# A fused delta-rule attention and soft mixture-of-experts kernel: second layer, slot sum, output products and stores by halves of the columns, with 128-row output products and 48 stores

## The chip, the core and the metric

The kernel runs on one core of one Trainium2 chip. The metric is the device time of one execution in microseconds (us); the figure to compare is the median of several runs. Engines are called as in the profile: PE (TensorE matmul), PEld (TensorE weight load), DVE (VectorE), ACT (ScalarE), POOL (GpSimd), SP (SyncE, which here only issues DMAs).

## The reference, cut to what matters

```python
# q, k, v: (4, 8, 768, 48), beta: (4, 8, 768)
for t in range(S):                                   # delta rule, one state per batch and head
    y[:, :, t] = einsum('bhd,bhde->bhe', q[:, :, t], state)
    v_old = einsum('bhde,bhd->bhe', state, k_n[:, :, t])
    state = state + bt * einsum('bhd,bhe->bhde', k_n[:, :, t], v[:, :, t] - v_old)
x = y.transpose(0, 2, 1, 3).reshape(3072, 384)
logits = x @ phi                                     # phi: (384, 32), 8 experts of 4 slots
slot_input = softmax(logits, axis=0).T @ x           # (32, 384)
for e in range(8):                                   # w1: (8, 384, 1024), w2: (8, 1024, 384)
    slot_out[e] = relu(slot_input[e] @ w1[e]) @ w2[e]
out = softmax(logits, axis=1) @ slot_out             # (3072, 32) @ (32, 384), float32
```

## The kernel before, in words

All arithmetic is float32. The sequence of 768 steps is cut into 12 chunks of 64 (`n`), taken in pairs (`g`). `get` loads k and q of a pair, transposes them on PE and forms Gram products (`gram`), which ACT copies out (`evP`, `evR`, `evB`, all through the helper `copy`, L178) and DVE masks (`mskA`, L365). `invert(g)` then solves a triangular system of the pair by many small DVE steps: it begins with one large transpose (`spread`, L383), goes through a reciprocal (L390) and a long row of `col` and `sub` steps, and ends with another transpose (`backT`, L447). `step(n)` carries the state from chunk to chunk on PE, ACT and DVE; `turn_y` and `route` make the logits, the running slot sums and the transposed combine weights `cT`. When all 12 chunks are through, the mixture-of-experts part follows, and this is where the change lies:

- `first` (L828): slot inputs times w1, for two groups of four experts (`qq`) and two halves of the hidden columns; `turnh` (L846) transposes the hidden layer.
- `second` (L862): hidden layer times w2. One call `snd{qq}.{u}` is 8 products of 384 columns, four experts side by side in four column groups of the array, all added into one PSUM bank `pso`. There are 8 calls.
- `evs` (L871, ACT) copies the bank out, `sum` (L873, PE) adds the four expert rows with a selection matrix, `so` (L874, DVE) divides by the softmax sums. The result is the 32 slots by 384 columns, four times over 32 rows each.
- `om` (L888, PE): the output product. Its weights are 96 columns of `cT` in one of four row groups of 32 rows, and 384 columns of `so` move: 8 calls of 4 products, each into a bank of its own, for 96 output rows each.
- `evo` (L893): 32 copies of 96x384 out of PSUM, half on ACT and half on DVE.
- `st` (L902): 16 stores of 96 partitions by 768 floats (two output rows that lie side by side, 3072 bytes), 10 issued by SP and 6 by POOL.

Every operation is recorded by name with its engine and then issued in an order written out as a table (`ORDER`); each engine takes its operations in that order and waits for what an operation needs. `BANKS` gives each PSUM tile its bank. The weight loads (names beginning with w, L776 and L817, all on SP) have a second table, `GATES`: a load waits besides for a named earlier operation. The lines of the tables' use:

```python
        for i in numbers(ORDER) or range(len(self.ops)):
            self.ops[i].fn()
            last[i] = tc.nc.cur_bb.bb.instructions[-1]
            if i in gates:
                tc.add_manual_dep(last[i], last[gates[i]].name, ...)
```

Of the kernel before, what the change touches and what calls it, by code (L numbers as in the profile page):

```python
# [17 lines left out]
    "#)##%x#&#-#%#3#+#*#(#2#,#'#$#E#D#=#F$K#6#>#.#?#7#G$e#@#O#A#B#C#8$|#P#H#<#4#Q#9#V#I#:#5#;#R#J$d#/#S#T"  # L18
    "#K#L$G#M#0#N$C#W$L$H$D$I#U$E$J$f#X$F#Y#Z$g#[$;#]#^$?#_&1$<#`$@#a$r#b#c$A$s#e#d$N#f#g#h$O%y#i$B$Y$P#j"
    "$=$Z#k#l$h#m$M$>$i$t#n$j#o&0$u#p#q$k$v#r#s#t$l#u&P$z#v$w#w$x#x$y#y$p${$m$n#z&Q$o#{%z$[#|%{#}$Q$q$]'~"  # L20
    "#~$^$#$R$$$%&2$&'}&3$'$S$b$_$`$a&l#1$($)$W&R$T$U&S$-$V$*&k$}'%$~$c%#%$%%%&%'%(%)%*%+%,$+$.%.%/%0%-%1"
    "(#%2%3%4%5%6%7%8&y%9$,%:$2$3%;&z%<%=$1%>%?&#$5%@$4%A%B%C%|&$%D&%$X&a%}(R%E$/%~%F&b%G%H(Q%I&&%J$0&(&'"
    "%K&T&)%L&*&U&V%M&+&_%N(t&,$8%O&`(s%P$6%Q&W%R$7%S(S%T&-%U$9&4$:%V&i&.%W&X&/%X%Y&c%Z&]&j&Y%[&Z%]&[&5&o"
    "&g%^&d&^)/&e&f%_)0&6&p%`&h&9%a&7&8%b%c&>%d&m%e&?%f&B%g&n&:&w&C%h*B&;%i&D%j&x%k%l($%m&<&I&q*A&=&H&@(%"
    "%n%o&K&v%s&{&A&u)E&r&E&|%u&}%t(r&F'$&G%v%w&~(;(q&s&t'#'&%p()%r%q&J''(*'(')'*(&*u'+','-)%(''.(w(('2'/"
    ")&*C'1(.+9(x)#*t(/(+'0'3'4'5(u'6(8'7'8(v+:(:'9(9':)3';(,'<(-(2)4'=)='>(3(0'?+R(4&L'@)>+Q'A&M'B(T*v)$"
    "'C'D(>(1'E(y(?'F'G'H(5(z'I({(U(|(}'J(~(V(6).'K(7'L)'(W'M(X'N(l)-)+'O)((_'P)))*'Q'R(`'S(c),(Y(d'T(e&N"
    "'U(Z*D&O'V,e(k'W*E+G'X)1+H'Y,d)2'Z);'[([)<']'^+='_(j'`(]-[(<(^'a(i-](a'b(='c(b(@'d+>'e'f)?(A'g(C(B'h"
    "'i(I(H(D)C'j(f(J)@'k)A(K'l(E)D(L(F'm(g+7(M'n)B(o'o(h(G)5(p'p'q(N+8*I)9'r)6(O)7)8(P*[*J's't)F'z-:'x+h"
    "'|'{-;)G*F):)H'y)I)J'u)K*G)L*H)M)N*K)R'v)O,f)P)Q*L*Y*M)S*_*X)T)U'w)V+;*`)W*N)X+<)Y*P)Z*O)[*Q)]*R)^+?"  # L30
    "*S)_)`*T)a*U+@)b+A*w-<)c+P+B)d*V+E)e*W*]+D+F)f+C+O*x*^+I)g)h*Z)i+M)j+J+U+K)k+L*y)l+V+N*|)m*z*{)n+%)o"
    "+^)p+&+S*}+_+))q/*+T)r*~+*)s++)t+W+#)u/++0)v+$)w+X+'+[)x,g+()y+/+,)z+Y+`){+--Z+]+1+a)|(m+Z+.)}+b(n)~"
    "-t,h-u,l*#+f*$+c-Y*a+d*%+e*&+i+5+6+3*'+41/*b*(,m*)+2/^+g-`**+j*+-j+k+l*,-a+m/]*--^-k+n*.-h*/-_+o*0-i"
    "*1+p*21-+q*3+r*4*5+s*6+t*<*9*8*7+v+w+x..+y,i*:+z+{*;*=+|+}+u+~,#,n,j,$,k/_,%,&,',(,q,),o*>,p,*,|,+,r"
    ",,*?,u,-*@,s,{,.-l,v,/,w,0,t,1-b-p,2-m-n,3/,-%-c,4,x-o,5-&-s,6,y-=,7,z-q-f-d,8-e-B-r,9->-#,:-$-C-'-g"
    "/}*c,;*e-(,<*d*g*f*k,=*h/|-)*i,>-,-+,?,~-*,@-1,A,}*j.$,B-?,C.%,D-x,E-@-v,F-A-y,G-G1,-w,H.&,I-H-D,J.'"
    ",K1.,L-z-R,M-Q,N,O-E.(-{,P-|,Q-},R-F,S-K.#.)-I.*,T.+,U-L./-M.,-~-U-J17-T,V-V.0.-.1-N.2.3-W10,W-O.4-2"
    ".5/--X,X-P-S16/2.6,_,[,Z/.11.7,Y/3,a,^.814.9,].:,`//0S,b,c.<*l.=/4/0.>/1.?*m0R.@.;.A/~.B.C.D.E/715.F"
    "/5.G/6/8.H/9/B.I--13/;/:.J/G-..K/<-/.L/H12.M/=/D.N/A.O/>.P/`/?1=.Q0T/@/C.R.S.T1;.U/a.V1</b.W.X.Y.Z.["
# [85 lines left out]
def kernel(  # L125
# [11 lines left out]
    nc = tc.nc  # L137
# [795 lines left out]
```

## Time and profile before

| | |
|---|---|
| median of 3 runs | 316.62 us (315.55 to 317.04) |
| the profiled execution | 319.18 us, of which the span of its instructions is 317.5 us |
| mean granted TensorE clock | 0.901 |
| busy in the span | PE 245.4, DVE 215.0, ACT 174.0, POOL 100.1 us |
| DMA | 45.08 MB, mean 142 GB/s; HBM written 4.72 MB (the output) |

The profile is one execution. Times in its views are counted from the span's start. Rows of the chain of waits give start, length and what ran; rows of a table of stretches give each engine's busy time in the stretch, with the count of instructions, then the granted clock, the share of time the 16 DMA engines were busy, and what they moved. In a timeline the bracket gives the idle time before an instruction and what ended it.

### The profile page before, as it was taken

How to read it: one execution, taken by the hardware profiler on the slowest of the kernel's cores; microseconds unless marked ns; L12 is line 12 of the kernel's file. 1: busy time of each engine (PE TensorE's matmuls, PEld its weight loads, DVE VectorE, ACT ScalarE, POOL GpSimd, SP SyncE). 2: the span in 40 equal slices, each digit the busy share in tenths (PEclk: the TensorE clock that was granted, in tenths of full speed). 3: DMA queues.
4: the chain of work that ended last, by engine and by line, in shares of the span. 5: the costliest groups of instructions: out<-in, count | busy, mean ns of one | idle time of the engine just before them, and what ended most of it. 6: DMA issues, size and time to landing. Idle time of an engine off the chain costs nothing.

```text
span 317.5 us, 13695 instructions
## 1 busy us (share of the span) xinstructions
PE 245.4 (77%) x5910; PEld 187.7 (59%) x5910; DVE 215.0 (68%) x584; ACT 174.0 (55%) x420; POOL 100.1 (32%) x215
## 2 busy tenths in 40 slices
PE   0768458879798887889759897787878988998930
PEld 0666347768786756678558586656747874343400
DVE  3378899996498989888899988848793306011630
ACT  1464824687777586878457677533448643201530
POOL 8920017354086005940069501690030000000210
PEclk9978956998999999999878997958879999999975
DMA  7989890395376264024930545966695789970396
GB/s 103 138 111 131 112 129 6 62 124 74 55 100 95 35 100 79 8 51 78 170 89 5 96 145 142 239 204 202 196 372 177 217 281 378 323 255 2 98 306 192
DMA packets 86956, 45.08 MB, mean 142 GB/s; under 512 B 78352, under 2 KB 78480, under 8 KB 86896
## 3 DMA queue, kind: packets, MB, share of 16 engines
q1 hardware_dynamic: 83856, 41.94, 58.5%
q0 software_dynamic: 896, 1.87, 2.2%
q8 instruction: 46, 0.75, 1.1%
q10 hardware_dynamic: 2144, 0.39, 1.0%
q14 instruction: 14, 0.11, 0.1%
HBM read 39.47 MB, written 4.72 MB: 139 GB/s over the span
## 4 chain that ended last, share of the span: by engine, by line
PE 56%; ACT 16%; DVE 8%; issue 6%; DMA 5%; SPq 4%; POOL 1%; POOLq 0%; DVEq 0%; ACTq 0%
ACT sb L178 15%; PE pb L571 6%; PE pb L621 6%; PE pb L327 5%; PE pb L588 5%; PE pb L559 4%; PE pb L862 3%; PE pb L828 3%; PE pb L346 3%; PE pb L495 3%; PE pb L888 3%; PE pb L602 3%; PE pb L469 2%; DMA sb<-in_q_dram 2%; PE pb L515 2%
## 5 line engine op out<-in xcount | busy, mean ns | idle before, releaser
L178 ACT ACTIVATE sb<-pb 128x384 f32<-128x384 f32 (+5 forms) x252 | 113.8, 467 | 72.0 <-PE pb L588 15.5
L531 POOL TENSOR_SCALAR sb<-sb 128x48 f32<-128x48 f32 x160 | 60.7, 405 | 23.9 <-DVE sb L412 14.2
L420 DVE TENSOR_TENSOR sb<-sb 128x31 f32<-128x31 f32 (+15 forms) x155 | 53.8, 347 | 4.3
L425 DVE TENSOR_TENSOR sb<-sb 128x31 f32<-128x31 f32 (+15 forms) x155 | 53.0, 342 | 4.4
L178 ACT ACTIVATE sb<-pb,sb 128x256 f32<-128x256 f32 (+1 forms) x96 | 39.7, 450 | 21.9 <-PE pb L571 7.8
L484 POOL TENSOR_SCALAR sb<-sb 128x512 f32<-128x512 f32 x10 | 16.6, 1667 | 91.9 <-DVE sb L447 23.2
L327 PE MATMUL pb<-sb 128*128 128x128 f32 x192 | 33.1, 317 | 13.0 <-DMA sb<-in_k_dram 9.0
L327 PEld LDWEIGHTS pb<-sb 128*128 128x128 f32 x192 | 24.8, 162 | 16.7 <-issue 10.4
L346 PE MATMUL pb<-sb 48*64 48x128 f32 (+1 forms) x896 | 28.6, 269 | 6.4 <-ACT sb L178 4.9
L571 PE MATMUL pb<-sb 64*64 64x48 f32 x768 | 28.9, 228 | 4.0 <-DVE sb L365 1.6
L571 PEld LDWEIGHTS pb<-sb 64*64 64x64 f32 x768 | 26.3, 143 | 6.7 <-DVE sb L365 1.8
L346 PEld LDWEIGHTS pb<-sb 48*64 48x64 f32 x896 | 23.5, 142 | 10.4 <-ACT sb L178 7.3
L515 PE MATMUL pb<-sb 64*64 64x48 f32 x768 | 29.1, 229 | 0.6 <-issue 0.6
L621 PE MATMUL pb<-sb 128*64 128x96 f32 x352 | 22.1, 274 | 6.8 <-ACT sb L178 4.0
L588 PE MATMUL pb<-sb 64*64 64x96 f32 x384 | 22.4, 258 | 6.2 <-issue 3.5
L515 PEld LDWEIGHTS pb<-sb 64*64 64x64 f32 x768 | 26.2, 143 | 0.8 <-issue 0.7
L621 PEld LDWEIGHTS pb<-sb 128*64 128x64 f32 x352 | 17.8, 152 | 12.1 <-ACT sb L178 4.7
L902 POOL DMA_DIRECT2D out_dram<-sb x6 | 3.2, 534 | 64.5 <-DVE sb L893 62.1
L588 PEld LDWEIGHTS pb<-sb 64*64 64x64 f32 x384 | 18.2, 140 | 8.8 <-ACT sb L178 4.3
L365 DVE TENSOR_TENSOR sb<-pb,sb 128x512 f32<-128x512 f32 x24 | 16.6, 690 | 9.2 <-ACT sb L178 7.8
L559 PE MATMUL pb<-sb 128*64 128x96 f32 x352 | 19.7, 254 | 3.2 <-ACT sb L178 2.0
L561 DVE TENSOR_TENSOR sb<-sb,pb 128x384 f32<-128x384 f32 x22 | 12.1, 552 | 11.1 <-PE pb L559 7.1
(114 smaller groups left out, 327.2 us busy)
## 6 DMA issues: line engine op xcount, KB each, us to landing
sb<-in_moe_w_dram SPq DMA_DIRECT2D x24, 512.0 KB, 5.0
sb<-in_moe_w_dram SPq DMA_DIRECT2D x32, 384.0 KB, 5.1
sb<-in_q_dram SPq DMA_DIRECT2D x24, 192.0 KB, 4.7
out_dram<-sb SPq DMA_DIRECT2D x10, 288.0 KB, 7.2
sb<-in_v_dram SPq DMA_DIRECT2D x24, 96.0 KB, 3.4
sb<-in_v_dram SPq DMA_DIRECT2D x48, 48.0 KB, 3.3
sb<-in_k_dram SPq DMA_DIRECT2D x22, 96.0 KB, 3.3
sb<-in_k_dram SPq DMA_DIRECT2D x44, 48.0 KB, 3.0
```

The costliest lines, as they stand in the source:

```text
L178: S_.activation(o, i, ACT.Copy, **kw)
L327: nc.tensor.transpose(F1(ps)[:, P * h:P * h + P], A(src)[:, x:x + P], ident())
L346: mm(A(ps)[ha(e), i, P * h:P * h + P].rearrange("p (a t) -> p a t", a=2)[:, pr[0]:pr[-1] + 1], x[hd(i), j, h, e], y[hd(i), j, h, e, pr[0]: ...
L365: V.tensor_tensor(o, x4(1), m.unsqueeze(1).unsqueeze(1).broadcast_to([P, 2, HQ, C]), op=ALU.mult)
L420: V.tensor_tensor(p(), v3(tt)[:, j:j + 1, 0:m].broadcast_to(sh), v3(lb)[:, j:j + 1, j + 1:32].rearrange("p x i -> p i x").broadcast_to(sh) ...
L425: V.tensor_tensor(t, t, p(), op=ALU.subtract)
L515: mm(F1(pY[n, j])[ha(1 - e), D * x:D * x + D], A(AA[n])[ha(e), a:a + C], A(UB[n])[ha(e), c:c + D], start=n == 0 and x == 0)
L531: G_.tensor_scalar(y, y, A(nb)[:, c:c + 1], 0.5, op0=ALU.mult, op1=ALU.mult)
L559: mm(bank(pK)[ha(e), j, 2 * D * h:2 * D * h + 2 * D], t4(n, 0)[:, j, 2 * b + h, e], bd()[:, j, b, h, e])
L571: mm(bank(pU[b])[ha(e), j, y:y + D], A(TW[g])[ha(e), a:a + C], A(R)[ha(e), c:c + D], start=x == 4 * b and j == 0)
L588: mm(bank(pU[b])[ha(e), :, y:y + D], A(BBb[g])[ha(e), a:a + C], A(U)[ha(e)].rearrange("p (j x d) -> p x j d", j=2, d=D)[:, x], start=False)
L621: mm(F1(pY[n, j])[ha(1 - e), 2 * D * h:2 * D * h + 2 * D], t4(n, 1)[:, j, h, e], bd()[:, j, h // 2, h % 2, e], start=h == 0)
```

## The change

1. `second` works on 192 columns at a time (`HC`), with a bank for each half (`pso[d]`, the two banks that held the state sums). There are 16 calls `snd{d}.{qq}.{u}`, and `evs`, `sum`, `so` exist once for each half. The table puts half 1 ahead of half 0.
2. `om{d}.{mp}.{cj}` has 128 columns of `cT` as weights and 192 columns of `so[d]` moving; two such products (`e`) stand side by side in one bank, both in the same row group `cj`. There are 24 calls of 2 products. `evE` writes `cT` in another order of columns for it, with the same number of elements.
3. `evo` is 24 copies of 128x384, 12 on ACT and 12 on DVE.
4. `st` is 48 stores of 128 partitions by 192 floats (768 bytes, half an output row each), 24 on SP and 24 on POOL.
5. `ORDER`, `BANKS` and `GATES` are new throughout, for the front of the kernel too.

The code, with the closing part of the old version left out:

```diff
-            A(cT).rearrange("p (x a q m) -> p m x q a", a=2, q=16, m=NG)[:, m],
-            F1(pe2)[:, 0:P].rearrange("p (x q a) -> p x q a", q=16, a=2)), r=[pe2], w=[(cT, m)])
+            A(cT).rearrange("p (e m y) -> p m e y", e=2, y=C)[:, m],
+            F1(pe2)[:, 0:P].rearrange("p (e y) -> p e y", e=2)), r=[pe2], w=[(cT, m)])
...
-    pso = pl.ps()
+    HC = Dm // 2
+    pso = [Buf(x, 1, True) for x in H2]
+    sj = [Buf(rt[1] + HC * x, HC) for x in H2]
+    so = [Buf(rt[0] + HC * x, HC) for x in H2]
+    obs = [Buf(w1b[e, kk].addr + Dm * x, Dm) for e in range(3, 7) for kk in range(NKT) for x in H2]
+    def second(qq, u, d):
         def prod():
             for t in (2 * u, 2 * u + 1):
                 for j in range(4):
-                    mm(F1(pso)[32 * j:32 * j + 32, 0:Dm],
+                    mm(F1(pso[d])[32 * j:32 * j + 32, 0:HC],
                        A(hTb[qq])[:, P * t + 32 * j:P * t + 32 * j + 32],
-                       A(w2b[4 * qq + j, u])[:, Dm * (t % 2):Dm * (t % 2) + Dm], start=qq == 0 and t == 0)
+                       A(w2b[4 * qq + j, u])[:, Dm * (t % 2) + HC * d:Dm * (t % 2) + HC * d + HC], start=qq == 0 and t == 0)
+    def put(d):
+        for qq in H2:
+            for u in range(4):
+                second(qq, u, d)
+        ACTO("evs%d" % d, HC, lambda: S_.copy(A(sj[d]), F1(pso[d])[:, 0:HC]), r=[pso[d]], w=[sj[d]])
+        p4 = pl.ps()
+        PE("sum%d" % d, 560, lambda: mm(F1(p4)[:, 0:HC], A(csel), A(sj[d])), rec=4, r=[csel, sj[d]], w=[p4])
+        DVE("so%d" % d, HC, lambda: V.tensor_scalar(
+            A(so[d]), F1(p4)[:, 0:HC], A(sS)[:, 3:4], None, op0=ALU.mult), r=[p4, (sS, 2)], w=[so[d]])
+        for mp in range(NG // 2):
+            for cj in range(4):
+                c, j = divmod(cj, 2)
+                po, ob = pl.ps(), obs.pop(0)
+                def om(mp=mp, cj=cj, po=po):
+                    r = slice(32 * cj, 32 * cj + 32)
+                    for e in H2:
+                        a = HD * e + P * mp
+                        mm(F1(po)[:, HC * e:HC * e + HC], A(cT)[r, a:a + P], A(so[d])[r])
+                PE("om%d.%d.%d" % (d, mp, cj), 340, om, rec=8, r=[cT, so[d]], w=[po])
+                (DVE if cj % 2 else ACTO)("evo%d.%d.%d" % (d, mp, cj), Dm, ..., r=[po], w=[ob])
+                for e in H2:
+                    def st(c=c, j=j, e=e, mp=mp, ob=ob):
+                        b = 2 * (1 - e) + j
+                        o = out[b * S:b * S + S, HC * d:HC * d + HC].rearrange("(m c y) d -> c m y d", c=2, y=C)
+                        (G_ if e else nc.sync).dma_start(out=o[c, 2 * mp:2 * mp + 2], in_=A(ob)[:, HC * e:HC * e + HC])
+                    DMA("st%d.%d.%d.%d" % (d, mp, cj, e), 0.9, st, 290, eng="POOL" if e else "SP", r=[ob])
+    for d in H2:
+        put(d)
```

Where the tables move instructions is shown at three places, as rows of an engine's order: line, operation, operands, shape, and how many of the kind stand in a row. The lines of the new version are one higher than the old ones up to L857 (L862 became L868, L873 became L880, L888 became L892, L902 became L900).

PE at the end of the program, before: second layer (L862), hidden transposes (L846), one transpose of `route` (L717), `sum` (L873), `om` (L888).

```order
L862 MATMUL pb<-sb 32x384 x8
L846 MATMUL pb<-sb 128x128 x4
L862 MATMUL pb<-sb 32x384 x24
L846 MATMUL pb<-sb 128x128 x4
L862 MATMUL pb<-sb 32x384 x16
L717 MATMUL pb<-sb 128x128
L862 MATMUL pb<-sb 32x384 x8
L873 MATMUL pb<-sb 128x384
L888 MATMUL pb<-sb 96x384 x32
```

The same place now, from the last hidden transpose on (L847), with the second layer L868, `sum` L880 and `om` L892.

```order
L847 MATMUL pb<-sb 128x128 x4
L868 MATMUL pb<-sb 32x192 x32
L880 MATMUL pb<-sb 128x192
L868 MATMUL pb<-sb 32x192 x8
L892 MATMUL pb<-sb 128x192 x12
L868 MATMUL pb<-sb 32x192 x16
L892 MATMUL pb<-sb 128x192 x4
L868 MATMUL pb<-sb 32x192 x8
L892 MATMUL pb<-sb 128x192 x2
```

Where all of `om` stood behind all of the second layer, the first `sum` now stands ahead of six of the eight calls of half 0 (8 products each), and the `om` products of half 1 stand between those calls. Behind these rows come 8 and 8 more products of the second layer, with 2 and 4 of `om` behind them, then the second `sum`, and last the 24 `om` products of half 0 in one row. The last transpose of `route` (`trE5`, L717 before) now stands ahead of the first layer.

DVE near the program's start, before: copies of the first transposes (L331), `spread` of pair 0 (L383), two masks (L365), the steps that follow.

```order
L331 COPY sb<-pb 128x512 x4
L383 STREAM_TRANSPOSE sb<-sb 128x1024
L365 TENSOR_TENSOR sb<-pb,sb 128x2x4x64
L387 TENSOR_SCALAR sb<-sb 128x32
L365 TENSOR_TENSOR sb<-pb,sb 128x2x4x64
L390 RECIPROCAL sb<-sb 128x32
```

The same place now.

```order
L332 COPY sb<-pb 128x512 x4
L366 TENSOR_TENSOR sb<-pb,sb 128x2x4x64 x2
L384 STREAM_TRANSPOSE sb<-sb 128x1024
L388 TENSOR_SCALAR sb<-sb 128x32
L391 RECIPROCAL sb<-sb 128x32
```

Both masks went ahead of `spread`, and with them what they need: the q transposes of chunk 1 and their Gram products.

ACT near the start, before: `evP` and `evR` (from PSUM alone, 128x2x4x32 and 32x2x4x32) and `evB` (with a scale from SBUF) of the four Gram products of pair 0, and `evT` of the q transposes of chunk 1 (128x512). `spread` reads what all `evP` and `evR` write.

```order
L178 ACTIVATE sb<-pb,sb 128x2x4x32 x2
L178 ACTIVATE sb<-pb 128x2x4x32
L178 ACTIVATE sb<-pb 32x2x4x32 x2
L178 ACTIVATE sb<-pb 128x2x4x32
L178 ACTIVATE sb<-pb 32x2x4x32 x2
L178 ACTIVATE sb<-pb 128x2x4x32
L178 ACTIVATE sb<-pb 32x2x4x32 x2
L178 ACTIVATE sb<-pb,sb 128x2x4x32
L178 ACTIVATE sb<-pb 128x512 x2
L178 ACTIVATE sb<-pb,sb 128x2x4x32
```

The same place now.

```order
L179 ACTIVATE sb<-pb,sb 128x2x4x32 x2
L179 ACTIVATE sb<-pb 128x2x4x32
L179 ACTIVATE sb<-pb 32x2x4x32 x2
L179 ACTIVATE sb<-pb 128x512
L179 ACTIVATE sb<-pb,sb 128x2x4x32
L179 ACTIVATE sb<-pb 128x512
L179 ACTIVATE sb<-pb 128x2x4x32
L179 ACTIVATE sb<-pb 32x2x4x32 x2
```

The last `evP` with its two `evR` stood ahead of two `evB` and two `evT`; now these four stand ahead of it.

More of the change, by code (lines that the diff above doesn't have):

```diff
@@ L23 @@
[L23 to L27, printed above, removed]
@@ L855 @@
         load_w2(qq)
-    pso = pl.ps()
-    def second(qq, u):
+    HC = Dm // 2
[4 more added lines that the diff above has]
+    def second(qq, u, d):
         def prod():
@@ new lines, in prod @@
+                       A(w2b[4 * qq + j, u])[:, Dm * (t % 2) + HC * d:Dm * (t % 2) + HC * d + HC], start=qq == 0 and t == 0)
+        PE("snd%d.%d.%d" % (d, qq, u), 820, prod, rec=32, r=[(hTb[qq], u // 2)] + [w2b[4 * qq + j, u] for j in range(4)],
+           w=[pso[d]])
+    def put(d):
[12 more added lines that the diff above has]
+                def om(mp=mp, cj=cj, po=po):
+                    r = slice(32 * cj, 32 * cj + 32)
+                    for e in H2:
+                        a = HD * e + P * mp
+                        mm(F1(po)[:, HC * e:HC * e + HC], A(cT)[r, a:a + P], A(so[d])[r])
+                PE("om%d.%d.%d" % (d, mp, cj), 340, om, rec=8, r=[cT, so[d]], w=[po])
+                (DVE if cj % 2 else ACTO)("evo%d.%d.%d" % (d, mp, cj), Dm, lambda po=po, ob=ob, cj=cj: (
+                    V.tensor_copy if cj % 2 else S_.copy)(A(ob), F1(po)[:, 0:Dm]), r=[po], w=[ob])
+                for e in H2:
[4 more added lines that the diff above has]
+                    DMA("st%d.%d.%d.%d" % (d, mp, cj, e), 0.9, st, 290, eng="POOL" if e else "SP", r=[ob])
```

104 lines of the change are left out of this document (38 added, 66 removed).

## The prediction

> **What bounds the kernel now.** I read the page first (busy shares, chain), then the chain of waits in order of time for the last 40 us, a table of stretches, the groups by line and shape, and a timeline of the start.
>
> ```profile
> PE 56%; ACT 16%; DVE 8%; issue 6%; DMA 5%; SPq 4%; POOL 1%; POOLq 0%; DVEq 0%; ACTq 0%
> 40.00:80.00 40.00, 32.37 (x1152) 28.70 (x1153) 34.62 (x85) 23.15 (x53) 17.77 (x36) 0.79 0.56 77
> 160.00:200.00 40.00, 33.23 (x874) 28.49 (x876) 35.39 (x90) 26.99 (x69) 20.24 (x37) 0.87 0.39 102
> ```
>
> Over the front no engine is quite full: in these two stretches DVE is the busiest, 34.6 and 35.4 of 40 us, and since its small steps depend on each other it is nearly full. The end is another matter.
>
> ```profile
> 278.19 1.29 PE pb L862 x16
> 279.48 0.64 PE pb L846 x4
> 289.83 1.47 PE pb L862 x16
> 291.38 0.49 ACT sb L871
> 291.91 0.93 PE pb L873 x2
> 292.86 0.63 DVE sb L874
> 293.54 2.48 PE pb L888 x16
> 297.30 15.78 SPq L902 DMA_DIRECT2D out_dram<-sb  x10
> 302.00:306.00 4.00, 2.23 (x13) 0.77 (x12) 2.15 (x5) 2.08 (x5) 1.40 (x3) 0.98 1.00 306
> 306.00:310.00 4.00, 0.00 (x0) 0.00 (x0) 0.00 (x0) 0.00 (x0) 0.16 (x1) 0.50 0.96 302
> 314.00:318.00 4.00, 0.00 (x0) 0.00 (x0) 0.00 (x0) 0.00 (x0) 0.00 (x0) 0.50 0.26 87
> ```
>
> PE runs the second layer from 278.19 to 291.3 without a gap; then `evs`, `sum`, `so` and `om` follow one another. The first store issues at 297.30. From 302 on the DMA engines are full (share 1.00 and 0.96, 306 and 302 GB/s), PE and the copies are done by 306, and the kernel only waits for 4.72 MB to be written. In the last stretch 87 GB/s for 4 us is 0.35 MB, 1.1 us at 306 GB/s, so data ends near 315.2 and 2.3 us of completion follow. So the last 20 us are bound by the stores, and before that by when they can start.
>
> **The change, term by term.** I keep the clock of the profiled execution and first let the front end where it did.
>
> *Second layer by halves.* A call before is 16 records in 1.29 to 1.47 us, four experts side by side, so four steps of 384 columns, about 0.33 us each. A half call has four steps of 192 columns: half of 1.36, 0.68 us, if the weight loads, now twice as many, stay hidden.
>
> ```profile
> 282.47 0.13 PEld L862 LDWEIGHTS pb<-sb 128*32 128x32 f32 x4 [0.19 <-issue]
> L888 PE MATMUL pb<-sb 32*96 32x384 f32 x64 | 10.4, 517 | 1.2 <-DVE sb L874 0.7 <-ACT sb L893 0.2 <-DVE sb L893 0.2
> L893 DVE COPY sb<-pb 96x384 f32<-96x384 f32 x16 | 8.1, 550 | 3.9 <-PE pb L888 3.9
> L893 ACT COPY sb<-pb 96x384 f32<-96x384 f32 x16 | 6.8, 478 | 6.6 <-PE pb L888 6.6
> L902 POOL DMA_DIRECT2D out_dram<-sb x6 | 3.2, 534 | 64.5 <-DVE sb L893 62.1 <-ACT sb L893 2.3
> ```
>
> Four loads take 0.13 us and then idle 0.19; a step of 0.16 us still covers them, barely. If it doesn't, a step costs 0.02 or 0.03 more, 1 to 2 us over 64 steps.
>
> *The first stores.* Ahead of the first `sum` stand ten half calls (eight of half 1, two of half 0) and three hidden transposes of 0.64: 6.8 + 1.9 from 278.2, so 286.9. Its copy `evs` hides under a call of half 0. `sum` and `so` at half width are about 0.5 and 0.4 us (0.93 and 0.63 above for 384 columns), so the first `om` starts at 287.9; two products of two passes each in one row group are four steps of 0.16, and a copy 0.5: the first store issues at 289.1, against 297.30. Before, data moved 1.2 us behind the first issue: the first row below cuts 297 to 299 into 40 slices of 0.05 us, and the DMA share leaves zero in the 32nd, at 298.55. So it would at 290.3. Nothing else wants the DMA engines then, if the w2 loads are in:
>
> ```profile
> DMA  0000000000000000000000000000000559967999
> 280.15 0.33 SPq L817 DMA_DIRECT2D sb<-in_moe_w_dram  x1
> sb<-in_moe_w_dram SPq DMA_DIRECT2D x32, 384.0 KB, 5.1
> ```
>
> The last w2 load issued at 280.15 and lands 5.1 us later by the median, 285.3; the call that needs the last load now comes at 285.5 instead of 289.83. Its gate is the second call of half 1, done at 280.2. So this cover is almost gone: I charge 0, and up to 1 us in the range.
>
> *The rest of PE.* From 287.9: five calls of half 0 (3.4 us; a sixth runs under `so`), and 12 `om`. Alone each is 0.65 us; neighbours in different row groups run side by side (the 4 products before did: 16 records, of two passes each, in 2.48 us, though a record takes 0.5 by itself). By the row groups in the table's order the five clusters take about 1.95, 0.65, 0.65, 0.65 and 0.65: 4.55 us, 7.8 if none overlap. `sum` of half 0 at 295.9, its `om` from 296.8 (300 at worst). Its 12 copies go six to an engine at 0.55: 3.3 us behind a first one, done near 301.4. The 24 copies, as wide as the old ones, are 12 at 0.478 and 12 at 0.550, 12.3 us, where 32 made 16.4; half of them now lie beside the second layer.
>
> *Stores.* Data can flow from 290.3, half of it before about 298. Issue: POOL took 0.534 us a store, 24 are 12.8 us, the 12 of half 0 from 298 end near 304.5; SP's issues before were slowed by full queues, and its shortest row, the load above, is 0.33. Neither is the bound. The bound is what 6144 rows of 768 bytes cost where 1536 of 3072 moved at 306 GB/s. No row shows 768 bytes. The ends:
>
> ```profile
> 0.00:40.00 40.00, 22.02 (x458) 18.46 (x461) 24.95 (x79) 20.61 (x47) 16.12 (x35) 0.91 0.98 119
> ```
>
> The first 40 us load q, k and v in rows of 192 bytes, at 119 GB/s with the engines full. At 119 the output would take 39.7 us, at 306 15.4. Per engine (a sixteenth, by busy share) that is 25 ns for 192 bytes and 161 ns for 3072; the line between them gives 52 ns for 768, 234 GB/s, 20.2 us. Loads issued one behind another may pay for more than their size, so I take 250 GB/s: 18.9 us, from 290.3 to 309.2. With 2.3 us of completion the span ends at 311.5, 6.0 us earlier. Bounds of this term: 307.9 at 306 GB/s (the copies end at 301.4 and would then nearly bind), 312.8 at 234.
>
> The Trainium skill, "DMA: Bandwidth & Descriptors", section "Why small descriptors are slow (HBM only)", states about 3 cycles of overhead a packet beside one cycle for 32 bytes. By that 768 bytes cost 27 cycles and 3072 cost 99, an estimate of 280 GB/s and 16.9 us, an end 2.0 us earlier than mine; it can't be the whole cost, for 192 bytes would lose only a third by it, and the row above lost more.
>
> *The new order of the front.* It is not free.
>
> ```profile
> 12.07 1.21 ACT L178 ACTIVATE sb<-pb 128x256 f32<-128x256 f32 x3 [10.00 <-PE pb L346]
> 18.10 1.07 ACT L178 ACTIVATE sb<-pb 128x512 f32<-128x512 f32 x2
> 19.05 0.50 ACT L178 ACTIVATE sb<-pb,sb 128x256 f32<-128x256 f32 x1
> 17.73 1.96 DVE L383 STREAM_TRANSPOSE sb<-sb 128x1024 f32<-128x1024 f32 x1 [3.04 <-ACT sb L178]
> 19.73 0.69 DVE L365 TENSOR_TENSOR sb<-pb,sb 128x512 f32<-128x512 f32 x1
> 24.14 1.06 PE pb L346 x32
> 21.16 0.34 DVE L390 RECIPROCAL sb<-sb 128x32 f32<-128x32 f32 x1
> ```
>
> `spread` of pair 0 starts at 17.73, as soon as ACT has made the last copy for it. Two copies of 0.53 and two of at most 0.50 now stand ahead: 2.0 us. It also waits for the second mask, which follows the second q copy (done near 18.5), a Gram product of near 1.06 us and takes 0.69 itself: 20.3, 2.6 us later. The two masks that used to follow are then done, and one of them filled the wait ahead of L390, so that comes at 23.2 instead of 21.16: 2.0 us late on the engine that is nearly full. Further on, two more masks and the next `spread` stand ahead of the second closing transpose of pair 0, which the state of chunk 0 waits for. Against that DVE has holes where a delay can vanish:
>
> ```profile
> DVE sb L365 <- ACT sb L178: 2.6, 1, 2.6
> DVE sb L383 <- ACT sb L178: 2.4, 1, 2.4
> 232.75 0.55 DVE L561 TENSOR_TENSOR sb<-sb,pb 128x384 f32<-128x384 f32 x1
> 233.22 1.97 DVE L447 STREAM_TRANSPOSE sb<-sb 128x1024 f32<-128x1024 f32 x1
> 234.05 1.43 PE pb L686 x8
> 235.49 1.48 PE pb L621 x16
> 236.97 2.32 PE pb L495 x64
> 235.02 0.28 DVE L704 TENSOR_TENSOR sb<-pb,sb 128x128 f32<-128x128 f32 x1
> 266.90 7.93 PE pb L828 x72
> ```
>
> The first two rows are waits between 70 and 90 us, 5.0 us together. The next rows are the close of DVE's part: the last `backT` ends at 235.19, and PE reaches what needs it (L495) at 236.97, being busy till then: 1.8 us to spare. The new table also puts eight small steps of `route` (like the row of L704, 0.28 us each, 2.2 us) ahead of that `backT`, and one state step (L561, 0.55) behind it. So 2.0 + 1.7 at `backT`, less 1.8 to spare, is 1.9 at the first layer, which began at 266.90 (L828). The holes can take some back, and the later state of chunk 0 can add some: bounds -3.1 (all of 5.0 taken back) and +4.5 (nothing closed, and the states late by another 2.6). I take +1.5, the sum with a little credit for the holes. The transpose of `route` moved ahead of the first layer displaces one that stood there, at the same 0.27: nothing.
>
> *Sum:* -6.0 + 1.5 = -4.5 us. The profiled execution was 319.18 with a span of 317.5, 2.56 above the median of 316.62. I take the difference over to the median: 312.1, rounded to 312.0.
>
> **Rivals.**
>
> *Stores at the full 306 GB/s.* The tail ends at 307.9, with the front's +1.5 the time is 308.5; without it 307.0. For it: a 768-byte row may cost just its bytes. Against: the row of 119 GB/s. The Trainium skill, "DMA: Bandwidth & Descriptors", section "Specifications", gives 512 bytes as the least transfer for line rate, by which this would be the outcome; no row here tests it. Chance 0.25, for 304.5 to 309.5.
>
> *The front eats it.* The lag at the first `spread` passes into the chain of states and no hole takes it back: +4.5 or more, with the tail at 311.5 or 312.8, gives 315.1 to 316.5, no change. For it: the closing transposes of pair 0 come later by more than `spread` did. Against: the holes. Chance 0.13.
>
> *Slower: rows of 768 bytes run nearer to the small loads.* Place: all 48 stores. Even the early start can't help when the queue lasts past the old end: with the front's +1.5, data must end by 313.7 to break even, 23.4 us from 290.3, 202 GB/s. At 180 GB/s it takes 26.2 us and the time is 319.4. For it: the same row, and two queues of small rows at once. Against: the line above gives 234. Chance 0.10. The Trainium skill, "DMA: Bandwidth & Descriptors", in a comparison of generations in the section "Why a DMA increments its semaphore by 16 and not by 1", names 2 KiB a partition as the least that saturates the DMA engines on earlier chips; by that 768 would not, and it speaks for this rival, without a price; no row here has a store of 2 KiB or less.
>
> **How the numbers follow.** My forecast has 0.45 (309.5 to 314.9), the first rival 0.25, the second 0.13, the third 0.10; the rest, 0.07, lies in parts of the order that I haven't followed, 0.05 of it faster and 0.02 slower. 0.5% of 316.62 is 1.6 us, about what can be told from no change. Faster: 0.45 + 0.25 + 0.05 = 0.75. Same 0.13, slower 0.12. The range runs from 305.5, inside the first rival, to 316.5, the end of the second, leaving out about 0.2.
>
> **What would show it.** First store near 289 plus the front's lag; DMA busy from there to the end, with no gap at the second `sum`; stores near 250 GB/s; 0.65 to 0.70 us for a call of 16 records at L868; `spread` of pair 0 near 20.3; the first layer's start at 266.9 + 1.5. It is wrong if the stores run below 200 GB/s, if DMA waits for the second half, if PE waits for w2 near 285, or if the first layer starts later than 270.

## The result, and the profile after

| | before | after |
|---|---|---|
| median | 316.83 us (315.55 to 318.16, 4 runs) | 371.5 us (370.25 to 372.54, 4 runs) |
| ratio, with its 95% interval | | 1.172 (1.166 to 1.179) |
| the profiled execution, its span | 319.18, 317.5 us | 371.27, 369.6 us |
| start of the second layer, in the span | 278.00 us | 276.50 us |
| from there to the end | 39.5 us | 93.1 us |

The change made the kernel 17% slower; 312.0 was forecast. Of the 52.1 us that the span grew, 53.6 lie behind the start of the second layer, and the front gives 1.5 back. (Ratios with an interval here and below leave out executions that ran disturbed; medians are over all runs.)

PE did what the change says. Timeline of PE after (start, us, what):

```profile
276.50 0.83 PE L868 MATMUL pb<-sb 128*32 128x192 f32 x16
...
279.33 2.81 PE L868 MATMUL pb<-sb 128*32 128x192 f32 x64
...
282.71 3.01 PE L868 MATMUL pb<-sb 128*32 128x192 f32 x64
285.65 0.59 PE L880 MATMUL pb<-sb 128*128 128x192 f32 x2
...
292.20 0.91 PE L892 MATMUL pb<-sb 32*128 32x192 f32 x4
...
297.42 6.80 PE L892 MATMUL pb<-sb 32*128 32x192 f32 x48 [0.51 <-DVE sb L881]
```

The first `sum` (L880) runs at 285.65 and the last `om` is done near 304. But the kernel ends at 369.6. The table of stretches says what happens in between (last two columns: share of time that the 16 DMA engines are busy, GB/s), and the timeline of SP's queue below it says who is at work:

```profile
300.00:310.00 10.00, 4.22 (x27) 3.71 (x23) 3.07 (x6) 1.88 (x5) 5.56 (x7) 0.53 0.45 87
310.00:320.00 10.00, 0.00 (x0) 0.00 (x0) 0.00 (x0) 0.00 (x0) 4.77 (x6) 0.50 0.34 68
...
340.00:350.00 10.00, 0.00 (x0) 0.00 (x0) 0.00 (x0) 0.00 (x0) 0.00 (x0) 0.50 0.14 47
...
360.00:370.00 10.00, 0.00 (x0) 0.00 (x0) 0.00 (x0) 0.00 (x0) 0.00 (x0) 0.50 0.11 36
...
288.42 73.61 SPq L900 DMA_DIRECT2D out_dram<-sb  x24
```

Nothing but SP's stores runs from 330 on, and they move 47 GB/s where the old stores moved 306. The column to read is the one beside it: the DMA engines are busy for 0.14 of the time, not 1.00. So the transfers are not slow because each row costs much on a busy engine; most engines have nothing to do. 0.14 of 16 engines is 2.2. The count of packets says the same. Here are the two hardware-queue lines, after first (288 to 370 us), then before (296 to 318 us): packets, MB, share.

```profile
q1 hardware_dynamic: 3120, 2.36, 9.7%
...
q1 hardware_dynamic: 1120, 2.95, 43.6%
```

After, 24 stores of 128 rows leave 3120 packets, 24 x (128 + 2); before, 10 stores of 96 rows leave 1120, 10 x (96 + 16). Beside its rows a store has one small packet for each engine that takes part: 16 engines before, 2 after. What differs is the shape of a store on the side of DRAM. Before it is `[c, g]` of "(m c u q a)", 16 (`q`) rows of 6 by 768 floats; now it is `o[c, 2 * mp:2 * mp + 2]`, 2 (`m`) by 64 (`y`) by 192 floats. The slowest dimension fell from 16 to 2. The Trainium skill, "DMA: Bandwidth & Descriptors", section "Why a DMA increments its semaphore by 16 and not by 1", states such a rule: a DMA is spread over the largest number of engines, up to 16, that divides the slowest dimension of both sides. That these counts follow it is shown by the experiments.

The rate of 2 engines is not the whole of the loss. SP's 24 stores are 2.36 MB, which is 50 us at 47 GB/s, but SP's row lasts 73.6 us. The two queues (q1 is SP's, q0 POOL's) from 290 to 330 us, then SP's from 330 to 370, when POOL's stores are done:

```profile
q1 hardware_dynamic: 832, 0.63, 7.1%
q0 software_dynamic: 4504, 2.42, 30.3%
...
q1 hardware_dynamic: 2274, 1.72, 12.7%
```

Beside POOL's stores SP's queue moved 0.63 MB in 40 us, 16 GB/s, a third of what it moves alone. At 47 GB/s it would have moved 1.25 MB more by 330, which is 27 us of the end (an estimate from these figures). What the two queues share there is not in the records.

POOL's queue suffers as well. POOL's line of stores after (ns, min/median/max), and what it waited for (us, times):

```profile
L900 POOL DMA_DIRECT2D out_dram<-sb x24: 796/796/878, 288.9 to 325.1; - x24
  DMA out_dram<-sb: 14.3, 10
```

An issue takes 0.796 us instead of 0.534, and POOL waits 14.3 us for earlier stores of its own.

### The profile page after: what moved, and what is told of

Read it like the earlier page. It is cut to its first block, busy times and chain, and to the rows that moved or that the text cites. A ratio compares the mean times of both kernels' runs of the same rounds, so it can differ in the third digit from the quotient of the medians.

```text
span 369.6 us, 14076 instructions
## 1 busy us (share of the span) xinstructions
PE 249.3 (67%) x6072; PEld 198.6 (54%) x6072; DVE 212.0 (57%) x581; ACT 171.4 (46%) x417; POOL 117.3 (32%) x233
## 3 DMA queue, kind: packets, MB, share of 16 engines
HBM read 39.47 MB, written 4.72 MB: 120 GB/s over the span
## 4 chain that ended last, share of the span: by engine, by line
PE 30%; issue 22%; DVE 15%; DMA 13%; ACT 4%; POOL 2%; SPq 2%; POOLq 0%; DVEq 0%; ACTq 0%
DMA out_dram<-sb 7%; PE pb L347 5%; PE pb L328 5%; ACT sb L179 4%; DMA sb<-in_k_dram 4%; DVE sb L421 3%; PE pb L572 3%; DVE sb L426 3%; PE pb L589 3%; DMA sb<-in_q_dram 3%; PE pb L560 3%; PE pb L496 2%; PE pb L470 2%; DVE sb L448 2%; PE pb L622 2%
## 5 line engine op out<-in xcount | busy, mean ns | idle before, releaser
L179 ACT ACTIVATE sb<-pb 128x384 f32<-128x384 f32 (+5 forms) x252 | 110.9, 464 | 46.5 <-PE pb L589 13.9
L532 POOL TENSOR_SCALAR sb<-sb 128x48 f32<-128x48 f32 x160 | 61.9, 413 | 34.0 <-DMA sb<-in_v_dram 19.0
L328 PE MATMUL pb<-sb 128*128 128x128 f32 x192 | 34.0, 319 | 15.1 <-DMA sb<-in_k_dram 9.8
L900 POOL DMA_DIRECT2D out_dram<-sb x24 | 19.1, 801 | 71.9 <-DVE sb L894 54.3
L328 PEld LDWEIGHTS pb<-sb 128*128 128x128 f32 x192 | 24.5, 161 | 20.3 <-issue 9.8
L347 PE MATMUL pb<-sb 48*64 48x128 f32 (+1 forms) x896 | 32.0, 290 | 4.8 <-ACT sb L179 4.1
L572 PE MATMUL pb<-sb 64*64 64x48 f32 x768 | 28.1, 226 | 5.0 <-DVE sb L562 2.5
L347 PEld LDWEIGHTS pb<-sb 48*64 48x64 f32 x896 | 26.0, 159 | 9.2 <-ACT sb L179 6.2
L572 PEld LDWEIGHTS pb<-sb 64*64 64x64 f32 x768 | 26.0, 142 | 7.0 <-DVE sb L562 3.6
L516 PE MATMUL pb<-sb 64*64 64x48 f32 x768 | 27.1, 220 | 3.3 <-issue 3.3
L516 PEld LDWEIGHTS pb<-sb 64*64 64x64 f32 x768 | 24.6, 134 | 3.7 <-issue 3.5
L589 PEld LDWEIGHTS pb<-sb 64*64 64x64 f32 x384 | 18.3, 140 | 9.4 <-ACT sb L179 4.9
L560 PE MATMUL pb<-sb 128*64 128x96 f32 x352 | 20.9, 265 | 1.7 <-ACT sb L179 1.7
L622 PE MATMUL pb<-sb 128*64 128x96 f32 x352 | 19.6, 255 | 1.1 <-ACT sb L179 1.0
L560 PEld LDWEIGHTS pb<-sb 128*64 128x64 f32 x352 | 16.8, 146 | 4.4 <-ACT sb L179 2.7
L622 PEld LDWEIGHTS pb<-sb 128*64 128x64 f32 x352 | 15.8, 139 | 5.0 <-issue 2.8
```

The lines of the kernel that those rows point to most:

```text
L179: S_.activation(o, i, ACT.Copy, **kw)
L328: nc.tensor.transpose(F1(ps)[:, P * h:P * h + P], A(src)[:, x:x + P], ident())
L347: mm(A(ps)[ha(e), i, P * h:P * h + P].rearrange("p (a t) -> p a t", a=2)[:, pr[0]:pr[-1] + 1], x[hd(i), j, h, e], y[hd(i), j, h, e, pr[0]: ...
L516: mm(F1(pY[n, j])[ha(1 - e), D * x:D * x + D], A(AA[n])[ha(e), a:a + C], A(UB[n])[ha(e), c:c + D], start=n == 0 and x == 0)
L532: G_.tensor_scalar(y, y, A(nb)[:, c:c + 1], 0.5, op0=ALU.mult, op1=ALU.mult)
L560: mm(bank(pK)[ha(e), j, 2 * D * h:2 * D * h + 2 * D], t4(n, 0)[:, j, 2 * b + h, e], bd()[:, j, b, h, e])
```

## The experiments

They ran on other chips of the same kind, on which the kernel before takes 313 to 316 us. The figure to compare in the profiles is the closing part, from the first product of the second layer to the end of the span, because it repeats: 39.5 us before, and 39.4 in a second profile.

| kernel | second layer starts | span | closing part |
|---|---|---|---|
| before; a second profile of it (e12) | 278.00; 272.88 | 317.5; 312.3 | 39.5; 39.4 |
| new front, old closing part (e11) | 276.34 | 315.3 | 39.0 |
| after | 276.50 | 369.6 | 93.1 |
| rows 64x2 (e1); the same behind the old front (e8) | 278.00; 271.39 | 315.4; 309.0 | 37.4; 37.6 |
| and each store behind its copy (e5) | 278.64 | 314.0 | 35.4 |
| and row groups in turn (e6); behind the old front (e9) | 277.32; 274.63 | 311.3; 308.7 | 34.0; 34.1 |
| and 5 stores moved to ACT, old front (e10) | 275.86 | 308.6 | 32.7 |

### Are the engines of a store the cause? (e1)

Same size of rows, same number of stores, same queues and order; only the order of the 128 rows in a store is turned, so that the dimension of 64 is the slow one.

```diff
-            A(cT).rearrange("p (e m y) -> p m e y", e=2, y=C)[:, m],
+            A(cT).rearrange("p (e b y z) -> p b z e y", e=2, y=C, z=2)[:, m // 2, m % 2],
...
-                        o = out[...].rearrange("(m c y) d -> c m y d", c=2, y=C)
-                        (G_ if e else nc.sync).dma_start(out=o[c, 2 * mp:2 * mp + 2], ...)
+                        o = out[...].rearrange("(b z c y) d -> c b y z d", z=2, c=2, y=C)
+                        (G_ if e else nc.sync).dma_start(out=o[c, mp], ...)
```

> The changed kernel with one thing altered: the 128 rows of an output product stand in the order (y, m) instead of (m, y), so a store's row dimensions in DRAM are 64x2 instead of 2x64. Same bytes, same 768-byte rows, same addresses, same 48 stores on the same queues. Theory (a store from SP is spread over only as many DMA engines as its slowest row dimension allows, 2 of 16; in the last 30 us of the changed kernel the DMA share was 0.13 to 0.14 and the rate 47 GB/s): all 16 engines work, stores run from 289.6, POOL's 24 issues of 0.80 us end near 308 and the span near 311, time 309 to 314. Rival 1 (768-byte rows are slow by themselves): no change, 371. Rival 2 (48 stores at once on two queues block each other): no change, 371.

Measured: 318.23 us median (315.93 to 322.1, 4 runs), the kernel before 315.79 beside it. The 53 us are gone. Its packets, landing of the stores (KB, us), and the GB/s in 40 slices of 285 to 316 us:

```profile
q1 hardware_dynamic: 3456, 2.36, 24.8%
...
out_dram<-sb SPq DMA_DIRECT2D x24, 96.0 KB, 2.3
out_dram<-sb POOLq DMA_DIRECT2D x24, 96.0 KB, 2.4
...
GB/s 0 0 0 0 0 0 0 1 248 216 236 162 271 282 200 269 181 244 141 274 282 200 127 186 242 206 0 261 193 246 254 302 331 287 246 38 0 0 0 0
```

3456 is 24 x (128 + 16): 16 engines. The 768-byte rows run at 302, 331 and 287 GB/s in three slices near the end, as fast as the 3072-byte rows did, and a store lands 2.3 us after its issue. Neither the size of the rows nor the number of stores was the cost. But the gain that was to follow isn't there: the closing part is 2.1 us shorter than before, not 6.0.

### The kernel before with 6 engines a store (e2)

The other direction: the old kernel, its stores of 3072-byte rows left whole, with the slow dimension made 6.

```diff
-            A(cT).rearrange("p (x a q m) -> p m x q a", a=2, q=16, m=NG)[:, m],
+            A(cT).rearrange("p (x a m q) -> p m x q a", a=2, q=16, m=NG)[:, m],
...
-                o = out[...].rearrange("(m c u q a) d -> c u q m (a d)", c=2, u=2, q=16, a=2)[c, g]
+                o = out[...].rearrange("(m c u q a) d -> c u m q (a d)", c=2, u=2, q=16, a=2)[c, g]
```

> The kernel before with the rows of an output product in the order (m, q) instead of (q, m), so a store's row dimensions in DRAM are 6x16 instead of 16x6. Same bytes, 3072-byte rows, 16 stores. Theory of the engine count: SP's ten stores use 6 engines. At 23.5 GB/s an engine (47 over 2) 2.95 MB take 20.9 us, 25.6 if POOL's stores load the same six with their share, from 298.5: span 321.7 to 326.4, time 321 to 326. Rivals 1 and 2 (row size, number of stores): no change, 316.8.

Measured: 335.9 us median (330.4 to 338.93), against 315.79. A stretch of it in which only SP's and POOL's stores are left, and its packets:

```profile
310.00:320.00 10.00, 0.00 (x0) 0.00 (x0) 0.00 (x0) 0.00 (x0) 0.00 (x0) 0.50 0.38 131
...
q1 hardware_dynamic: 1020, 2.95, 20.3%
...
out_dram<-sb POOLq DMA_DIRECT2D x6, 288.0 KB, 18.2
```

0.38 is 6/16, and 1020 is 10 x (96 + 6). The cause is shown from both sides, on two kernels and at two row sizes. The price was 20 us rather than the 4 to 9 expected: POOL's stores had been taken to spread over all 16 engines, but one landed 18.2 us after its issue by the median, where 6.8 was the figure before.

### Which queue pays: all on SP (e3), all on POOL (e4)

```diff
-                        (G_ if e else nc.sync).dma_start(out=o[c, 2 * mp:2 * mp + 2], ...)
+                        nc.sync.dma_start(out=o[c, 2 * mp:2 * mp + 2], ...)      # e3
+                        G_.dma_start(out=o[c, 2 * mp:2 * mp + 2], ...)           # e4
```

> The changed kernel with all 48 stores issued by SP, still 2x64 rows. Theory of the engine count: 4.72 MB over 2 engines at 47 GB/s take 100 us from 289.6, span 392, time 394. Rival 1 (row size): the same bytes in the same rows, no change, 371. Rival 2 (two queues block each other): faster than 371, one queue alone.

> The changed kernel with all 48 stores issued by POOL, still 2x64 rows. Theory of the engine count, with POOL's queue spread over all engines (its stores ended by 327 in the changed kernel though they shared two engines with SP's): bound by 48 issues of 0.80 us, 38.4 us from 288.9, the last landing some 5 us later: span near 332, time 334. If POOL's stores too had only 2 engines: 394. Rival 1: no change, 371.

Measured: e3 392.34 us, e4 368.06 us (one run each). A stretch and the packets of e3; below them a stretch of e4, POOL's stores in it and its wait for them:

```profile
330.00:340.00 10.00, 0.00 (x0) 0.00 (x0) 0.00 (x0) 0.00 (x0) 0.00 (x0) 0.50 0.14 46
...
q1 hardware_dynamic: 6240, 4.72, 13.0%
```

```profile
330.00:340.00 10.00, 0.00 (x0) 0.00 (x0) 0.00 (x0) 0.00 (x0) 5.54 (x7) 0.50 0.42 77
...
L900 POOL DMA_DIRECT2D out_dram<-sb x48: 796/796/881, 292.6 to 355.5; - x48
  DMA out_dram<-sb: 21.8, 21
```

e3 is as expected: 48 x (128 + 2) packets, 47 GB/s, all 4.72 MB at that rate. e4 is a miss. POOL's software queue had been thought to spread any store over all 16 engines; it moves 65 to 79 GB/s. Its packets show how a store is split: 98,304 bytes leave 22 packets of data, twice 10 of 4608 bytes and one of 3072, and each of these two sets is half of the store (49,152 bytes), as two engines would share it. Beside them stand 140 packets of 24 bytes and 14 of 16, fourteen more sets of eleven with next to nothing in them, as for the fourteen engines left over. That is read from sizes; the records don't name the engine. A DMA share of 0.36 to 0.42 in most stretches, about a quarter of it in the small packets, says that more than one such store was at work at a time. What holds the queue to 65 to 79 GB/s all the same is open. The same section of the Trainium skill excepts some direct copies of the software queue from the rule and gives them all 16 engines; by these sizes the stores here are not among them. So both queues split such a store in two, and moving the stores from one to the other doesn't mend it.

### The order of the stores (e5) and of the row groups (e6)

With the rows at 64x2, what holds the closing part? In e1 the timelines of POOL and PE show the end of it:

```profile
298.92 6.39 PE L892 MATMUL pb<-sb 32*128 32x192 f32 x48 [0.51 <-DVE sb L881]
...
306.38 4.92 POOL L900 DMA_DIRECT2D out_dram<-sb  x8 [0.92 <-ACT sb L894]
```

POOL issues its last 8 stores in a row only when the last copy is done, since a store early in its order needs a late copy; and `om` of half 0 takes 6.39 us. e5 puts each store right behind its copy. e6 also takes the 12 `om` of a half with the row groups 0, 1, 2, 3 in turn and six banks in turn, two things at once. Names in `ORDER` behind `sum0`:

```diff
-sum0 st1.1.3.1 st1.0.0.0 so0 ... om0.1.2 om0.1.0 ... om0.0.2 evo0.1.2 ... om0.2.2 om0.2.1 ... st0.1.2.0 evo0.1.1 ...
+sum0 so0 om0.1.2 om0.1.0 om0.0.2 evo0.1.2 st0.1.2.0 st0.1.2.1 om0.2.2 om0.2.1 ...                     # e5
+sum0 so0 om0.0.0 evo0.0.0 st0.0.0.0 st0.0.0.1 om0.0.1 evo0.0.1 st0.0.1.0 st0.0.1.1 om0.0.2 ...        # e6
```

> The (y, m) version with one more thing altered: each queue's stores stand in the order of the copies they wait for. In the (y, m) version POOL's last 8 stores went out back to back from 306.4, 0.62 us each, because the fifth of its 12 stores of half 0 waits for the last copy of all (ended 305.8). Theory (the store queues' order holds the end back): last issue about 1 us behind the last copy, span 4 us shorter than 315.4, so near 311, and the time 4 us below that of the (y, m) version in the same state. Rival (the DMA engines or their completion set the end): no change.

> The version with ordered stores, and besides the output products of each half in the order of the row groups 0, 1, 2, 3, three times, with banks 2 to 7 in turn (before, up to three neighbours shared a row group; their copies alternate ACT and DVE now). Theory (same row group in succession keeps PE from running products side by side, and copies from alternating): the 12 products of half 0 take about 4.5 to 5 us in place of 6.4, the time 1.5 to 2 us below the version with ordered stores. Rival (weight loads of 0.184 us or the copies bind whatever the order): no change to that version.

Measured: e5 317.32 us median of 10, ratio 1.013 (1.004 to 1.022); e6 316.61 us of 10, ratio 0.994 (0.990 to 0.998). The same two places in e6:

```profile
297.69 3.53 PE L892 MATMUL pb<-sb 32*128 32x192 f32 x48 [0.51 <-DVE sb L881]
...
299.42 7.37 POOL L900 DMA_DIRECT2D out_dram<-sb  x12 [0.73 <-ACT sb L894]
```

The closing part falls by 2.0 us with e5 and another 1.4 with e6, where `om` of half 0 takes 3.53 us instead of 6.60. Of e5 twice as much was expected (4 us); POOL's last 10 stores still stood in one row there, 6.14 us from 303.44. In e6 POOL's 12 stores of the last half stand in one row of 7.37 us, 0.614 each: POOL's issue has become the end. The timed runs show little of this: e5 lies above the kernel before by its whole interval, e6 0.2% to 1.0% below it.

### The front and the closing part apart (e7, e8)

```diff
-ORDER, BANKS, GATES of the changed kernel throughout
+e7: those of the changed kernel up to the first layer, then the closing part of before
+e8: those of before up to the first layer, then the closing part of e1
```

> The kernel before from the first layer on, behind the new order of everything ahead of the first layer. Measures the front alone. The changed kernel began its first layer at 264.3 and the (y, m) version at 265.2, the kernel before at 266.9: if the new front is worth that, the time is 1.7 to 2.6 us below the kernel before. If the first layer's own stretch (9.0 and 9.6 us for 72 records, against 7.9) also comes from the new order of loads, 0 to 1 us. My prediction's step (the front costs 1.5): 1.5 us above.

> The (y, m) version from the first layer on, behind the old order of everything ahead of it. Measures the tail alone. From the first layer's start to the end the (y, m) version took 50.2 us and the kernel before 50.6: 0.4 us below the kernel before; 2 us below it if the first layer's slower stretch belongs to the front. My prediction's sum for the tail with all 16 engines (6 us gained) would be 6 us below.

Measured: e7 319.32 us median of 4 (312.67 to 322.14), spread too widely to say anything, so that it was run again (e11). e8 315.38 us median of 10, ratio 0.993 (0.988 to 0.998). With the old front the closing part of e1, shorter by 1.9 us, is worth about 2 by this ratio (the medians over all runs, 315.38 and 315.37, don't show it); with the new front it was worth nothing. That pointed to the front, against the profile, in which the changed kernel reaches its second layer 1.5 us earlier than before.

### The front again, and the best version (e9 to e12)

e9 is the old front with the closing part of e6. e10 takes from it the last stores of half 0, four of POOL's and one of SP's, and lets ACT issue them behind its last copy. e11 is e7 again with more runs; e12 is the kernel before, unchanged.

```diff
+    LATE = ((0, 1, 3, 1), (0, 2, 1, 1), (0, 2, 2, 1), (0, 2, 3, 0), (0, 2, 3, 1))
...
-                        (G_ if e else nc.sync).dma_start(out=o[c, mp], ...)
+                        {"POOL": G_, "ACT": S_, "SP": nc.sync}[q].dma_start(out=o[c, mp], ...)   # e10
```

> Old front with the tail of the run whose row groups follow in turn (rows of a store 64x2, each store behind its copy). Theory (store spread settled, the tail is worth 3 to 4 us against the old one, 46.8 us from the first layer's start to the end against 50.6, and the front order is worth nothing or little): 311 to 313 us by the median of undisturbed runs, 2 to 4 below the kernel before in the same runs. Rival (the front of the new order is what made its best run): no gain over the kernel before, 315.

> As the run beside it, but five of the last twelve stores of half 0 are issued by ACT behind its last copy (4 from POOL, 1 from SP), so POOL issues 20 and SP 23. Theory (POOL's issues, 0.617 us each and back to back, set the end of the stores): POOL's last row ends 2.5 us earlier (4 issues), the end 1 to 2 us earlier than in the run beside it, limited by the data then left. Rival (the data rate sets the end): no difference, within 0.5 us.

> The changed front with the closing part of before, a second time with more runs. Theory of the prediction (the moved masks and spread delay the front by 1.5 us): 1 to 2 us above the kernel before in the same runs. Rival (DVE's holes take it all back): equal within 1 us. What the trace of the changed kernel suggested (first layer 2.6 us earlier): 2 to 3 us below.

> The kernel before, unchanged, with a second profile: how far the start of the first layer differs between two profiled executions of the same program. If profiles repeat to within 1 us it starts at 266 to 268 again, and a shift of the front of 1.5 us can be read from a profile; if it starts several us away, as the old front did behind the new tail (258.9), it can't, and only timed runs tell.

| | median | ratio to before |
|---|---|---|
| before | 313.15 us (23 runs) | |
| e9 | 312.32 us (12 runs) | 0.994 (0.989 to 0.999) |
| e10 | 310.91 us (12 runs) | 0.993 (0.989 to 0.998) |
| e11 | 319.2 us (6 runs) | 1.020 (1.014 to 1.026) |
| e12 | 314.05 us (1 run) | |

e11 shows that the new order of the front costs time, 4.5 to 8.1 us by these timed runs (1.4% to 2.6% of 313), more than the prediction's 1.5. The size is less sure than that interval. e6 (new front) and e9 (old front) have the same closing part and the same ratio to the kernel before, 0.994; by their medians over all runs (316.61 against 315.37, and 312.32 against 313.15) the new front costs 0.7%, about 2 us. e9 carries a wait of 1.9 us of its own, shown below, which hides as much of the difference. DVE's rows for the masks and `spread` of pair 0, after first, then in e11 (its lines are numbered 35 lower), then in e12:

```profile
20.47 1.51 DVE L366 TENSOR_TENSOR sb<-pb,sb 128x512 f32<-128x512 f32 x2 [4.81 <-PE pb L347]
21.90 1.94 DVE L384 STREAM_TRANSPOSE sb<-sb 128x1024 f32<-128x1024 f32 x1
...
21.92 1.95 DVE L349 STREAM_TRANSPOSE sb<-sb 128x1024 f32<-128x1024 f32 x1
...
18.37 1.98 DVE L383 STREAM_TRANSPOSE sb<-sb 128x1024 f32<-128x1024 f32 x1 [2.86 <-ACT sb L178]
```

DVE idles 4.81 us for the Gram products and `spread` comes 3.5 us later than in e12. e12 also shows why the first profile misled: the same program reaches its second layer at 278.00 us in one profiled execution and at 272.88 in the other, on two chips whose medians differ by 3.7 us (316.83 and 313.15). A shift of 1.5 us there can't be read from one pair of profiles; only timed runs tell.

e10 against e9: POOL's last row, ACT's issues, and the stretch of the last stores, e9 first.

```profile
296.80 7.37 POOL L900 DMA_DIRECT2D out_dram<-sb  x12 [0.73 <-ACT sb L894]
300.00:305.00 5.00, 0.00 (x0) 0.00 (x0) 0.00 (x0) 0.00 (x0) 4.17 (x7) 0.75 0.91 282
```

```profile
298.02 4.91 POOL L902 DMA_DIRECT2D out_dram<-sb  x8 [0.73 <-ACT sb L895]
301.36 4.68 ACTq L902 DMA_DIRECT2D out_dram<-sb  x5
300.00:305.00 5.00, 0.00 (x0) 0.00 (x0) 0.43 (x1) 0.00 (x0) 2.94 (x5) 0.62 0.97 298
```

POOL's row is 2.46 us shorter, the DMA engines are full in the last stretch (0.97), and the closing part is 1.4 us shorter, as expected. In the timed runs the medians differ by 1.4 us too, but the intervals of the ratios overlap, so that a gain of e10 over e9 isn't shown. By their intervals both are faster than before, by 0.1% at the least and 1.1% at the most.

The closing parts of e9 and e10 are 5.3 and 6.7 us shorter than that of e12, and the timed gain is about 2 us. In their profiles the second layer starts 1.8 and 3.0 us later than in e12, and a wait on PE makes up much of that. PE at the start of the first layer in e9, then in e12:

```profile
261.75 0.45 PE L718 MATMUL pb<-sb 128*128 128x128 f32 x1 [1.88 <-DVE sb L715]
262.13 9.32 PE L829 MATMUL pb<-sb 128*32 128x512 f32 x72
...
260.04 0.45 PE L717 MATMUL pb<-sb 128*128 128x128 f32 x1
260.58 9.13 PE L828 MATMUL pb<-sb 128*32 128x512 f32 x72
```

e8, e9 and e10 have the old order of the front, but with `trE5` ahead of the first layer. There it waits 1.88 us for DVE (1.78 in e8, 1.87 in e10), and the first layer with it. In e12 `trE5` runs inside the second layer, at 284.38, without a wait. A version of e9 with `trE5` left at its old place was not run, so it isn't shown that these 1.9 us can be had. e10's first layer besides took 10.17 us for e12's 9.13; why is open.

## Why the prediction was wrong, step by step

- **The step that failed: "The bound is what 6144 rows of 768 bytes cost".** It priced the stores by the size of their rows alone, between 119 and 306 GB/s, and took the 16 engines for granted. The old rows of 306 GB/s were rows of a store that is spread over 16; the new store is spread over 2. From the first issue to the end it took 81.2 us (288.42 to 369.6), where 22.4 were forecast (289.1 to 311.5). At 2 engines the rate is 47 GB/s, outside both ends. Row size, which the step was about, turned out to cost nothing that these runs show: two engines move 23.5 GB/s each with 768-byte rows, where 16 moved 306 / 16 = 19.1 each with 3072-byte ones, and 16 engines with 768-byte rows reach 298 GB/s at a share of 0.97 (e10). That the two queues would hold each other up, some 27 us of the loss by the estimate above, the step left out as well. The diff had shown the cause, `[c, 2 * mp:2 * mp + 2]` with two rows of 64 where 16 stood.
- **The rival that ended slower** had the right side and the wrong mechanism: rows near the rate of the small loads. e1 rules it out, for it keeps the rows and loses the 53 us. The "full 306 GB/s" rival was right on the price of a row once the spread was mended.
- **"Neither is the bound"**, on the issues of POOL and SP: right for the changed kernel only because the data was so slow. With the stores mended, POOL's issues are what ends last (7.37 us in a row), where one took 0.617 us with rows of 64x2 and not 0.534. Even at 0.534 twelve in a row would be 6.4 us.
- **The 12 `om` of half 1 in 4.55 us** ("7.8 if none overlap"): 5.91 after, in five clusters of 2.23, 0.93, 0.91, 0.91 and 0.93 us, where 1.95 and four times 0.65 were forecast. That products of different row groups overlap was right; a single `om` of 4 records was mis-sized, 0.91 instead of 0.65. In the groups of after its weight loads are long, 32 rows by 128 columns at 208 ns, while those of the second layer, 128x32, take 109; that they are the reason was not tested.

```profile
L892 PEld LDWEIGHTS pb<-sb 32*128 32x128 f32 x96 | 10.7, 208 | 2.3 <-DVE sb L881 1.1 <-ACT sb L894 0.6 <-DVE sb L894 0.3
L868 PEld LDWEIGHTS pb<-sb 128*32 128x32 f32 x204 | 5.9, 109 | 2.9 <-issue 1.1 <-DVE sb L849 0.4
```

- **`om` of half 0 and its copies, 296.8 to 301.4**: `om` alone took 6.80 us, from 297.42. The granted clock (the number before the DMA share), 1.00 from 297 to 300, fell there:

```profile
300.00:302.00 2.00, 2.00 (x18) 2.00 (x17) 0.96 (x2) 0.91 (x3) 1.12 (x2) 0.67 0.56 109
302.00:304.00 2.00, 2.00 (x13) 1.71 (x9) 1.52 (x4) 0.48 (x1) 1.26 (x2) 0.50 0.43 82
```

  In e6, with the row groups in turn, `om` of half 0 took 3.53 us and was done at 301.22, with the clock at 1.00 to the end. So its gain over e5 is that of the order and of the clock together; no run parts them.
- **The half call, 0.68 us**: right. Two rows of four took 2.81 and 3.01 us, 0.70 to 0.75 each. The first store issued at 288.42, 11.9 us behind the start of the second layer; 10.9 was forecast (289.1 less 278.2).
- **The w2 loads, "0, up to 1 us"**: 0. PE runs through the 64 products at 282.71 without a gap.
- **The front, +1.5**: the sign is borne out by e11's timed runs, the size was too small by them (4.5 to 8.1 us, at or beyond the bound of +4.5), and the mechanism is shown only at its start. `spread` was put at 20.3 and came at 21.90. What becomes of the lag is open: against e12, e11 is 3.5 us late at `spread`, 1.3 at the last `backT` (229.81 for 228.49) and 3.0 at the first layer (263.54 for 260.58). The sign that was given for it, a first layer that starts at 266.9 + 1.5, did not appear in the profile after, where it starts at 264.31.
- **The sum**: the -6.0 us of the closing part can be had in a profile, but not from this version. It needs the rows turned (2.1 us below before), the stores behind their copies (2.0 more), the row groups in turn (1.4) and less on POOL (1.4): from 39.5 to 32.7 us with the old front. Of these 6.8 us about 2 show in the timed runs.

## What to carry to other kernels

Before a DMA is priced by its bytes, look at the shape of both sides: in these runs an outermost dimension of 2, 6, 16 and 64 put 2, 6, 16 and 16 of the 16 DMA engines to work. So make it a multiple of 16, and in a profile read GB/s beside the DMA engines' busy share (47 GB/s at 0.14 is an idle machine, not a slow row). When a stage is moved forward, check the tables that move with it by a timed hybrid of old and new, because two profiles of the same front, each some 275 us long and on two chips, lay 5 us apart. And once the transfers are quick, count the issues: a queue that issues 12 stores at 0.6 us each in a row is the next bound.

## What was not expected of the hardware

- POOL's software queue does not spread such a store either. With rows of 2x64 all 48 stores moved 65 to 79 GB/s from 300 us on, and one landed 10.6 us after its issue by the median, where 64x2 gave 2.4 us.
- The time in which POOL issues a store depends on its shape: 0.534 us for 16x6 rows, 0.598 for 6x16 (e2), 0.617 for 64x2, 0.796 for 2x64. ACT took 0.94 us an issue at the end of e10 (4.68 us for 5), with the DMA engines full.
- The two engines of SP's stores gave 23.5 GB/s each, more than the 19.1 that each gave when all 16 were at work. Beside POOL's stores SP's queue moved 16 GB/s, for 47 alone.
